# Attention at a quarter of its rate during the half-size products, from batch 2 on

## The chip, the cores and the metric

The kernel runs on one core of a Trainium2 chip. The metric is the device time of one execution in microseconds, as a median of several runs. The work is spread over five engines, each with its own queue of instructions that it goes through in order: PE (TensorE, the matmuls; its weight loads are shown apart as PEld), DVE (VectorE), ACT (ScalarE), POOL (GpSimd), and SP, which issues most of the DMA transfers.

## What is computed

Sigmoid attention over 8 batches, 12 heads, 448 positions and a head size of 64, and behind it a two-layer network over the 3584 tokens:

```python
scores = scale * np.matmul(q, k.transpose(0, 1, 3, 2)) - np.log(S)
attn = 1.0 / (1.0 + np.exp(-scores))
attn_out = np.matmul(attn, v)
x = attn_out.transpose(0, 2, 1, 3).reshape(B * S, H * D)      # 3584 x 768
h = x @ w_in                                                  # 768 x 2048
g = np.where(h >= 1, h, np.where(h <= -1, 0.0, (h + 1) ** 2 / 4))
out = g @ w_out                                               # 2048 x 768
```

## The kernel before

**Precision.** From a certain point on every float32 operand is split into a high and a low float16 part, scaled by a power of two; a product is then three matmuls (high by high, high by low, low by high). A split is an ACT instruction for the high part and a DVE (or POOL) instruction for the low one.

**Attention** is cut into pieces. A pair of heads has 3 full pieces (128 keys) and a smaller one (64 keys), so a batch has 6 x 4 = 24 pieces. `step(i)` moves attention on: it issues the scores of pieces ahead (`scores`, L435, L430, L449, into a `psc` tile, of which there are two), the sigmoid of each and its split (`weigh`: L478 and L486 on ACT, L487 on DVE), and the matmuls with v for pieces whose sigmoids are older (`av`, L524). In the later batches two pieces go in one step. At the last piece of a head pair ACT copies the result to `x32` (L533) and DVE takes its maximum (L534). `step` also loads the inputs of a later head pair (`raw`, L329, issued by SP), takes their maxima on ACT (`dump`, L345) and splits them on POOL (L381 to L383).

**The network** of batch b runs while the attention of batch b + 1 does. From batch 2 on the first layer is done by seven products of half-size blocks for each of 8 pairs of output chunks (`up_blocks`, L718: 9 matmuls of 224 columns in a unit, 56 units). Sums and differences of the seven come from DVE (L727) and ACT (L730, L736), and `bend` makes the nonlinear function and its split (L765, L768 on ACT, L766, L767, L769 on DVE). The second layer (`down`, L788: 6 matmuls of 448 columns in a unit, 48 units, 288 matmuls a batch) has one eviction for every 48 matmuls (L801, DVE).

**Between two batches** the x operands have to be built from `x32`. `start_blocks` takes the maximum over the batch (L556) and sets it on a diagonal (`diag`, L163, DVE); `finish_blocks` sums that on PE (L173, into a `psc` tile), takes the maximum (L174, DVE), makes the scale (L129 to L137, DVE), the block differences (L567, L569 on DVE; L568, L570 on POOL), and seven splits (L573 on ACT, L574 on DVE) in the order of the products. The first half-size product of the next batch reads the first split's two parts.

**What sets the order.** The loop over the units of a batch (L941) runs attention steps ahead of a unit while fewer have been made than the unit's share; `share` is the running sum of a weight for each unit. Only the first `last` = 92 of 104 units have a share; ahead of the unit with number `last` stands `start_blocks`, and behind it `finish_blocks`. A scheduler then places the instructions of each engine by priority (the order in which the program issues them) and by when it estimates them to be ready, so that the matmuls of later units can stand ahead of an attention step whose inputs it expects late.

## Time and profile before

| | |
|---|---|
| median of 3 runs | 1179.57 us (1179.01 to 1179.93) |
| profiled execution | 1178.28 us |
| its span in the profile | 1176.4 us |
| granted PE clock, mean | 0.996 |
| half-size products of batch 3, in the trace | about 520 to 600 us |
| down products of batch 3, last ones without attention | about 600 to 658 us |
| half-size products of batch 7, no attention beside them | 1068 to about 1125 us |

A row of the timeline gives start and length in us, the engine, the line of the kernel, what is written and read, a count, and in brackets the idle time before it and what ended it. A row of the stretches gives each engine's busy time in the stretch, with its instructions in parentheses, then the granted PE clock (1.00 is full), the share of the DMA engines and their GB/s. A matmul's length includes the time in which it overlaps the next one. A row of the waits gives the engine and line that waited, the engine and line that ended the wait, the total in us, how often, and the longest. A "pair" in what follows is a step of two pieces; a "boundary" is the place between two batches' networks.

### The profile page before, as it was taken

The page shows a single profiled execution, that of the slowest core. Times are in us where ns is not written, and L with a number is a line of the kernel's source. Part 1 is how long each engine was busy: PE and PEld are TensorE (multiplying, and loading weights), DVE is VectorE, ACT ScalarE, POOL GpSimd, SP SyncE. Part 2 cuts the span into 40 slices and gives each one's busy share as a digit, 9 for nine tenths or more (in the row PEclk, how much of TensorE's full clock was granted, in tenths as well). Part 3 has the DMA queues.
Part 4 walks back from the last instruction along what each step waited for, and adds up shares of the span by engine and source line. Part 5 has one row for each costly group of instructions (what it writes and reads, how often), then busy time and mean ns, then how long its engine had stood idle before and what let it go on. Part 6 is the DMA issues. An engine that isn't in the chain of part 4 may idle for free.

```text
span 1176.4 us, 20214 instructions
## 1 busy us (share of the span) xinstructions
PE 1123.5 (96%) x7662; PEld 672.0 (57%) x7662; DVE 813.2 (69%) x1730; ACT 722.9 (61%) x1199; POOL 289.3 (25%) x367
## 2 busy tenths in 40 slices
PE   8899999999988999999999999999999999999998
PEld 2244334454444775468744786448754687558954
DVE  6888976769868786368854788357873688646820
ACT  6878977568656766447763777456864576533410
POOL 0000000000334533424244235232533342310000
PEclk9999999999999999999999999999999999999999
DMA  9924553162564554216633264414562255302300
GB/s 360 399 81 149 161 155 95 44 211 87 189 204 151 195 189 155 72 57 203 237 110 100 81 228 171 140 56 143 192 212 64 65 197 179 129 17 107 145 17 31
DMA packets 58273, 170.00 MB, mean 145 GB/s; under 512 B 8641, under 2 KB 40001, under 8 KB 52033
## 3 DMA queue, kind: packets, MB, share of 16 engines
q1 hardware_dynamic: 56448, 159.29, 39.7%
q10 hardware_dynamic: 1728, 9.44, 2.3%
q8 instruction: 60, 0.98, 0.3%
q14 instruction: 37, 0.29, 0.1%
HBM read 126.94 MB, written 23.40 MB: 128 GB/s over the span
## 4 chain that ended last, share of the span: by engine, by line
PE 48%; DVE 16%; ACT 14%; DMA 9%; issue 5%; POOL 5%; SPq 2%; POOLq 0%; DVEq 0%; ACTq 0%
PE po L788 24%; PE ph L718 9%; PE ph L752 6%; DMA raw<-qkv 5%; PE pav L524 5%; DVE ahl L487 4%; ACT psc L478 4%; DVE xhl L727 3%; ACT ahl L486 2%; DVE g L766 2%; PE psc L435 2%; DVE g L767 2%; DMA w_out_sb<-w_in 2%; ACT ghl L768 2%; ACT dump L345 2%
## 5 line engine op out<-in xcount | busy, mean ns | idle before, releaser
L788 PE MATMUL po<-ghl,w_out_sb 128*128 128x448 f16 x2304 | 445.4, 353 | 7.7 <-ACT ghl L768 6.3
L788 PEld LDWEIGHTS <-w_out_sb 128*128 128x128 f16 x2304 | 222.6, 98 | 223.0 <-issue 21.0
L718 PE MATMUL ph<-w_in_sb 128*128 128x224 f16 x3024 | 302.6, 260 | 19.9 <-DVE xhl L727 16.6
L718 PEld LDWEIGHTS <-w_in_sb 128*128 128x128 f16 x3024 | 287.4, 98 | 38.6 <-issue 35.4
L487 DVE SCALAR_TENSOR_TENSOR ahl<-psc,ahl 128x896 f16<-128x896 f32 (+1 forms) x170 | 153.1, 901 | 100.1 <-ACT ahl L486 98.3
L381 POOL TENSOR_SCALAR raw<-raw,qkv_s 128x448 f32<-128x448 f32 (+1 forms) x93 | 75.7, 827 | 455.2 <-DVE qkv_i L137 395.9
L478 ACT ACTIVATE psc<-psc,nls,sqk 128x896 f32<-128x896 f32 (+1 forms) x136 | 128.1, 966 | 54.6 <-PE psc L449 34.5
L486 ACT ACTIVATE ahl<-psc 128x896 f16<-128x896 f32 (+1 forms) x170 | 125.9, 763 | 38.4 <-DVE ahl L487 37.3
L345 ACT ACTIVATE dump<-raw 128x448 f16<-128x448 f32 (+1 forms) x105 | 61.9, 589 | 88.7 <-DMA raw<-qkv 87.6
L752 PE MATMUL ph<-xhl,w_in_sb 128*128 128x448 f16 x576 | 112.7, 353 | 3.6 <-ACT xhl L547 1.8
L768 ACT ACTIVATE ghl<-g 128x448 f16<-128x448 f32 x128 | 73.0, 573 | 59.7 <-DVE g L767 58.9
L769 DVE TENSOR_TENSOR ghl<-g,ghl 128x448 f16<-128x448 f32 x128 | 84.0, 659 | 33.2 <-ACT ghl L768 32.6
L727 DVE TENSOR_TENSOR xhl<-ph,xhl 128x224 f32<-128x224 f32 x240 | 87.1, 384 | 18.0 <-PE ph L718 12.8
L752 PEld LDWEIGHTS <-w_in_sb 128*128 128x128 f16 x576 | 55.1, 98 | 62.9 <-issue 11.1
L765 ACT ACTIVATE g<-xhl,hr,ihr 128x448 f32<-128x448 f32 x96 | 68.4, 756 | 35.8 <-DVE xhl L727 34.5
L524 PE MATMUL pav<-ahl,v 128*64 128x448 f16 x748 | 88.0, 360 | 0.0
L766 DVE SCALAR_TENSOR_TENSOR g<-g,rk 128x448 f32<-128x448 f32 x112 | 81.2, 735 | 8.2 <-ACT g L765 8.0
L801 DVE TENSOR_SCALAR o<-po,od 128x448 f32<-128x448 f32 x42 | 28.5, 680 | 73.4 <-PE po L788 73.2
L435 PE MATMUL psc<-qk 128*128 128x448 f16 x252 | 62.5, 357 | 8.8 <-DVE ahl L487 5.5
L383 POOL TENSOR_TENSOR hl<-raw,hl 128x448 f16<-128x448 f32 x62 | 67.7, 1112 | 0.0
L767 DVE SCALAR_TENSOR_TENSOR g<-xhl,ihs,g 128x448 f32<-128x448 f32 x96 | 66.8, 708 | 0.3
L458 POOL COPY w_in_sb<-hl 64x128 f16<-64x128 f16 x68 | 27.9, 411 | 142.2 <-DVE hl L377 140.2
(151 smaller groups left out, 1120.3 us busy)
## 6 DMA issues: line engine op xcount, KB each, us to landing
w_in_sb<-blocks SPq DMA_DIRECT2D x48, 1344.0 KB, 6.8
raw<-qkv SPq DMA_DIRECT2D x34, 704.0 KB, 4.5
qk<-hl SPq DMA_DIRECT2D x320, 56.0 KB, 2.0
w_out_sb<-w_in SPq DMA_DIRECT2D x16, 768.0 KB, 11.1
out_t<-o SPq DMA_DIRECT2D x48, 224.0 KB, 1.9
blocks<-mixs SPq DMA_DIRECT2D x8, 768.0 KB, 3.5
w_out_sb<-w_out ACTq DMA_DIRECT2D x6, 768.0 KB, 5.4
raww<-w_out ACTq DMA_DIRECT2D x6, 768.0 KB, 6.2
```

Source lines behind the costliest of these rows:

```text
L435: once(nc.tensor.matmul(out, kq[:, j, 1, w], kq[:, j, 0, :], start=True, stop=False))
L478: nc.scalar.activation(a, a, AF.Sigmoid, bias=nls, scale=sqk)
L486: nc.scalar.activation(hi, x, AF.Copy, scale=ATT)
L487: made.setdefault(i, []).append(nc.vector.scalar_tensor_tensor(out=lo, in0=x, scalar=ATT, in1=hi, op0=ALU.mult, op1=ALU.subtract))
L524: once(nc.tensor.matmul(pav[j * D : (j + 1) * D, :S], *terms[j][t], start=c == 0 and t == 0, stop=mid and t == len(terms[j]) - 1,))
L718: nc.tensor.matmul(out, w[:, wt, wh, c * P : (c + 1) * P], xc[:, xt, c, xh, :], start=j in (0, 2) and c + wh + xh == 0, stop=c == HC - 1 a ...
L727: add = lambda out, q, other: nc.vector.tensor_tensor(out=out, in0=quarter(q), in1=other, op=ALU.add)
L752: nc.tensor.matmul(ph[:, :S], w_in_sb[:, f, wh, c * P : (c + 1) * P], xhl[:, c, xh, :], start=c == 0 and wh + xh == 0, stop=c == NCC - 1 a ...
L766: nc.vector.scalar_tensor_tensor(out=g, in0=g, scalar=rt, in1=g, op0=ALU.min, op1=ALU.mult)
L767: nc.vector.scalar_tensor_tensor(out=g, in0=h, scalar=ihs, in1=g, op0=ALU.mult, op1=ALU.max)
L768: latest["g"] = nc.scalar.activation(hi, g, AF.Copy)
L788: nc.tensor.matmul(po[:, :S], w_out_sb[:, f, wh, m * P : (m + 1) * P], ghl[:, f, gh, :], start=f == lo and wh + gh == 0, stop=f == hi - 1 ...
```

## The change

The weight of a unit is now 2 instead of 8 for the first 56 units of each batch from 2 on, which are the units of the half-size products; the 36 down units behind them that have a share keep 8. Batches 0 and 1 are as they were.

```diff
-DW = 8
+DW, UW = 8, 2
...
-        share = [DW // 2 if b < SB and u < NA * NCC // 2 else DW for u in range(last)]
+        mixed_up = 7 * NFC // 2 if b >= SB else 0
+        share = [UW if u < mixed_up else DW // 2 if b < SB and u < NA * NCC // 2 else DW for u in range(last)]
         share = [sum(share[:u]) / sum(share) for u in range(last + 1)]
```

NFC is 16, SB is 2. No instruction is added or removed; the scheduler's order changes from batch 2 on.

PE around the boundary from batch 2 to batch 3, before: the last attention matmuls with v (L524), down matmuls (L788), the sum of the diagonal (L173), and more down matmuls.

```order
L524 MATMUL pav_4839<-ahl_4834,v_4483 64x448
...
L788 MATMUL po_4878<-ghl_94,w_out_sb_91 128x448
...
L788 MATMUL po_4997<-ghl_94,w_out_sb_91 128x448
L173 LDWEIGHTS one_96 [waits DVE_49]
L173 MATMUL psc_5033<-diag_5025,one_96 128x128 [waits PE_49]
L788 LDWEIGHTS w_out_sb_91
...
L788 MATMUL po_5131<-ghl_94,w_out_sb_91 128x448
...
L435 MATMUL psc_5185<-qk_4723 128x448 [waits PE_49]
```

Between the last L524 and L173 stood 50 down matmuls, and 63 between L173 and the next scores (L435); at the later boundaries 49, 49, 49 and 36 ahead of it and 53, 53, 53 and 66 behind it.

The same place now:

```order
L524 MATMUL pav_4885<-ahl_4880,v_4621 64x448
...
L435 MATMUL psc_4960<-qk_4787 128x448 [waits DVE_49]
...
L449 MATMUL psc_4960<-hl_4776 128x448
L173 LDWEIGHTS one_96 [waits DVE_49]
L173 MATMUL psc_5033<-diag_5025,one_96 128x128 [waits PE_49]
...
L435 MATMUL psc_5185<-qk_4787 128x448 [waits PE_49]
...
L524 MATMUL pav_5207<-ahl_4968,v_4777 64x448 [waits Activation_49]
...
L430 MATMUL psc_5188<-hl_4776,w_in_sb_90 128x448 [waits DVE_49]
...
L157 MATMUL psc_5188<-mb_5192,one_96 128x3
...
L718 MATMUL ph_5221<-w_in_sb_90 128x224 [waits Activation_49]
...
L718 MATMUL ph_5221<-w_in_sb_90 128x224 [waits DVE_49]
```

All 288 down matmuls of the batch now stand ahead of L173, and behind it stand only scores and matmuls with v of the next batch's first pieces, then the products, whose first matmuls wait for the first split (ACT for its high part, DVE for its low one). The scores of the batch's last two pieces stand 12 matmuls L524 and 26 matmuls L788 ahead of the last L524; at the next boundaries 34, 25, 11 and 7 matmuls L788.

DVE at the same place now:

```order
L534 TENSOR_REDUCE xm_3510<-x32_92 128x1 [waits Activation_49]
L569 TENSOR_TENSOR xhl_93<-x32_92,xhl_93 128x672
L556 TENSOR_REDUCE xm1_5023<-xm_3510 128x1 [waits DVE_49]
L487 SCALAR_TENSOR_TENSOR ahl_4968<-psc_4957,ahl_4968 128x896 [waits PE_49,Activation_49]
L163 TENSOR_SCALAR diag_5025<-ident_98,xm1_5023 128x128 [waits DVE_49]
L487 SCALAR_TENSOR_TENSOR ahl_4972<-psc_4960,ahl_4972 128x896 [waits PE_49,Activation_49]
L174 TENSOR_REDUCE xm1_5023<-psc_5033 128x1 [waits PE_49]
```

Both L487 of the next batch's first two pieces stand inside the chain from L534 to L174; before, one of them stood ahead of L556 and the other ahead of L534.

PE at the boundary from batch 6 to batch 7 now, where no next pieces exist:

```order
L788 MATMUL po_11818<-ghl_94,w_out_sb_91 128x448
...
L524 MATMUL pav_11627<-ahl_11618,v_11413 64x448 [waits Activation_49]
...
L173 LDWEIGHTS one_96 [waits DVE_49]
L173 MATMUL psc_11720<-diag_11712,one_96 128x128 [waits PE_49]
...
L718 MATMUL ph_11870<-w_in_sb_90 128x224 [waits Activation_49]
...
L718 MATMUL ph_11870<-w_in_sb_90 128x224 [waits DVE_49]
```

Before, 66 down matmuls stood between L173 and L718 here; now none.

## The prediction

> **What bounds the kernel now.** I read the page first, then stretches of the timeline, then TensorE's waits. The page:

> ```profile
> PE 1123.5 (96%) x7662; PEld 672.0 (57%) x7662; DVE 813.2 (69%) x1730; ACT 722.9 (61%) x1199; POOL 289.3 (25%) x367
> ```

> TensorE (PE) works 96% of the span. The change alters no instruction, only the order, so it can move nothing but PE's idle time and its clock. The stretches show where that idle time is: the half-size products of batch 3 (520 to 600 us), its down products while attention runs (604 to 645), the last down products (645 to 658), the next products, and those of batch 7, which have no attention beside them.

> ```profile
> core 0: us, PE busy (x) PEld busy (x) DVE busy (x) ACT busy (x) POOL busy (x), PEclk, DMA share, GB/s
> 520.00:600.00 80.00, 78.09 (x699) 61.16 (x696) 65.79 (x139) 58.73 (x104) 34.67 (x44) 1.00 0.51 174
> 604.00:645.00 41.00, 40.59 (x230) 19.99 (x230) 16.53 (x34) 19.09 (x31) 17.46 (x24) 1.00 0.25 75
> 645.00:658.00 13.00, 13.00 (x78) 6.62 (x75) 9.03 (x29) 8.64 (x15) 0.71 (x1) 1.00 0.18 69
> 1068.00:1125.00 57.00, 55.44 (x543) 51.81 (x542) 40.42 (x86) 23.90 (x46) 0.00 (x0) 1.00 0.34 126
> ```

> DVE is 82% busy in the products and 40% in the down products. The idea has a basis: attention sits where DVE is short. But PE loses only 1.9 of 80 us there. PE's waits from 360 us on, and four of its gaps:

> ```profile
> PE ph L718 <- DVE xhl L727: 16.6, 8, 5.7
> PE po L788 <- ACT ghl L768: 6.3, 4, 2.7
> PE ph L718 <- ACT xhl L736: 1.6, 1, 1.6
> PE ph L718 <- DVE g L766: 1.6, 1, 1.6
> PE po L788 <- DVE xhl L727: 0.9, 4, 0.2
> ...
> 379.98 1.84 PE L718 MATMUL ph<-w_in_sb 128*128 128x224 f16 x9 [5.65 <-DVE xhl L727]
> 412.44 3.46 PE L718 MATMUL ph<-w_in_sb 128*128 128x224 f16 x18 [2.35 <-DVE xhl L727]
> ...
> 604.29 8.77 PE L788 MATMUL po<-ghl,w_out_sb 128*128 128x448 f16 x44 [1.24 <-ACT ghl L768]
> ...
> 1091.24 25.19 PE L718 MATMUL ph<-w_in_sb 128*128 128x224 f16 x261 [1.56 <-DVE g L766]
> ```

> In all 27.0 us. The 5.65 at the start of batch 2 (the order ahead of it is the same in both kernels) and the 1.56 of batch 7 (no attention) stay, so **the most that thinner attention can win is 27.0 - 5.65 - 1.56 = 19.8 us**.

> **The change part by part.** Steps come in pairs of pieces. Before, 24 pieces spread evenly over 92 units: a pair every 7.7 units, 8 of 12 pairs in the 56 product units. Now the weights are 56x2 + 36x8 = 400: a pair every 16.7 units, then every 4.2 units, 4 pairs and 8. But the order does not follow: in the down products the scheduler sets 41 to 45 matmuls between pairs, as it did before, not the 25 that 4.2 units would be. So attention slips towards the end of the batch and uses up all 288 down matmuls. Before, 53 to 66 of them stood behind `diag` and covered the building of the next batch's x operands (copy, maxima, scale, splits). Now none do, at each of the five boundaries from 2->3 to 6->7. Down products with pairs 42 matmuls apart ran without a new gap in the 604 to 645 row, so I cost that density at nothing; its cover is exactly that spacing.

> *First wait at a boundary.* What covered this chain, and how long its parts last (boundary 3->4 of the kernel before):

> ```profile
> 624.29 0.36 PE L449 MATMUL psc<-hl 64*128 64x448 f16 x2
> 624.59 1.32 PE L524 MATMUL pav<-ahl,v 128*64 128x448 f16 x12
> 625.85 7.93 PE L788 MATMUL po<-ghl,w_out_sb 128*128 128x448 f16 x41
> 626.00 0.58 ACT L345 ACTIVATE dump<-raw 128x448 f16<-128x448 f32 x1 [7.52 <-DMA raw<-qkv]
> ...
> 628.03 1.67 ACT L478 ACTIVATE psc<-psc,nls,sqk 128x448 f32<-128x448 f32 x2
> ...
> 633.03 0.63 DVE L487 SCALAR_TENSOR_TENSOR ahl<-psc,ahl 64x448 f16<-64x448 f32 x1 [0.60 <-ACT ahl L486]
> ...
> 637.88 0.63 ACT L533 ACTIVATE x<-pav,sqk 128x448 f32<-128x448 f32 x1
> ...
> 645.46 10.19 PE L788 MATMUL po<-ghl,w_out_sb 128*128 128x448 f16 x53
> ```

> The scores of the last two pieces end at 624.65; the pieces are ready at 633.66, 9.0 us later, of which 3.4 go to the `dump` that waits for its load ahead of the sigmoids in ACT's queue. A down matmul costs 7.93/41 = 0.193 us. For the rest of the chain the trace has one near double, boundary 1->2, with the same DVE order, the two L487 of the next batch's pieces in it:

> ```profile
> 358.58 0.62 DVE L534 TENSOR_REDUCE xm<-x 128x1 f32<-128x448 f32 x1 [0.96 <-ACT x L533]
> ...
> 362.84 1.09 DVE L487 SCALAR_TENSOR_TENSOR ahl<-psc,ahl 128x896 f16<-128x896 f32 x1 [0.34 <-ACT ahl L486]
> ...
> 365.62 1.90 DVE L574 SCALAR_TENSOR_TENSOR w_in_sb<-x,x_s,w_in_sb 128x672 f16<-128x672 f32 x1
> 367.56 0.90 DVE L574 SCALAR_TENSOR_TENSOR w_in_sb<-xhl,x_s,w_in_sb 128x672 f16<-128x672 f32 x1
> ...
> 368.98 5.35 PE L718 MATMUL ph<-w_in_sb 128*128 128x224 f16 x54
> ...
> 373.98 0.20 DVE L582 TENSOR_SCALAR qq<-qm 128x1 f32<-128x1 f32 x1
> ```

> From L534 to the end of the first L574 it took 8.9 us; with that L574 at 0.9, as its successor, 7.9. With the copy L533 (0.6 and 0.1 to pass on) the first product can run 8.6 us after the last attention matmul.

> - 2->3: behind the last scores stand 12 attention matmuls and 26 down matmuls, 1.3 + 5.0 = 6.3 us; then a half pair of scores and six of the ten last attention matmuls, about 1.3 together; the other four must wait for 9.0: 1.4 us idle. Then 8.6 us of chain, under which stand only the next pieces' scores and 12 attention matmuls, about 3.7 us: 4.9 idle. Together 6.3.
> - 4->5, 25 down matmuls: 6.5. 3->4, 34 of them: no first part, 4.9. 5->6, only 11: 15 fewer, 2.9 more than the first: 9.2.
> - 6->7: no next load and no next pieces. Ready 5.6 us from the sigmoids on (628.03 to 633.66) against 1.3 + 7x0.193 + 0.7 = 3.4: 2.2 idle; chain 8.6 less the two L487 and their wait, 2.5, so 6.1 bare. 8.3.

> Sum 35.2 us. From below: if the next pieces' L487 slip behind the chain and the load is early, 6.1 - 3.7 = 2.4 four times and 6.1 once, 16. From above: the load as late as at its worst in the waits of ACT, 8.8 instead of 7.5 us, and an L574 of 1.9 each time, some 45. I keep 35, from the near double.

> ```profile
> ACT dump L345 <- DMA raw<-qkv: 81.2, 15, 8.8
> ```

> *Second wait.* From the end of the first L574 (367.52) the six other splits and the scales keep DVE until 374.18, 6.7 us; behind them stand the two L487 of the next pieces and the L727 on which the fifth product waits, some 2 us more; PE's 54 matmuls last 5.35. So PE waits again, up to 3.4 us, and 1.5 at 6->7, where no L487 is. One L727 now stands ahead of the L487, which helps. Bounds: 0, and the 5.65 us of batch 2. I take 3 four times and 1.5: 13.5.

> *The clock.* After the gap of 5.65 us PE came back slow:

> ```profile
> 378.00:380.00 2.00, 0.02 (x1) 0.02 (x1) 1.94 (x12) 1.36 (x5) 0.00 (x0) 0.60 0.00 0
> 380.00:382.00 2.00, 2.00 (x11) 1.45 (x10) 1.91 (x8) 0.58 (x3) 0.00 (x0) 0.50 0.00 0
> 382.00:384.00 2.00, 2.00 (x10) 0.66 (x10) 0.69 (x6) 1.12 (x2) 1.51 (x3) 0.50 0.03 8
> 384.00:386.00 2.00, 2.00 (x12) 0.54 (x9) 0.23 (x1) 1.07 (x3) 2.00 (x4) 0.69 0.00 0
> ...
> 414.00:416.00 2.00, 2.00 (x12) 1.51 (x10) 0.90 (x4) 0.00 (x0) 0.00 (x0) 0.51 0.49 197
> ```

> The granted clock was 0.50, 0.50 and 0.69 over six us: 1.0 + 1.0 + 0.6 = 2.6 us lost. Five boundaries: 13; from 0 to twice that, if the second wait slows it once more.

> [...]

> *What is won.* Up to 19.8 us, and 2 of clock behind the 2.35 us gap. The order has 5 pairs in the products where there were 8: six pieces of about 1.1 us on DVE each, 6.6 of its 65.8 us, go. Batch 7 shows that gaps remain even without attention (1.56), and the gap at 604.29 comes of a load. I take two thirds: 13.

> Sum against the profiled execution (span 1176.4, with 1.9 around it 1178.3): +35.2 + 13.5 + 13 - 13 = +48.7. The median of the three runs is 1.3 above that execution: **1179.6 + 48.7 = 1228 us**.

> **The rivals.**
> *Faster.* The chain shrinks to its lower bound at all boundaries, 16 us, the second wait is hidden under the products' 5.35 us, the clock drops only at 6->7 (2.6), and 21.8 are won: -3, 1176 us. It decides for itself only if a boundary costs less than 4 us. For it: the pieces' 9.0 us contain 3.4 of waiting for a load. Against: the first product's matmuls wait for ACT and DVE in the order with nothing but attention ahead, and 1->2 shows the chain at its length. 0.05.
> *Deeper.* With more pairs in the down products the loads arrive later each time, ACT stands before `dump` up to 8.8 us with the sigmoids behind it, and the second wait is 5.65 each time: +10 + 15 + 8 of clock on the forecast, 1260. For it: 81.2 us of such waits on ACT already. Against: the spacing that sets them is unchanged. 0.14.
> *It doesn't do what it says.* The weights shift pairs that the scheduler puts back by readiness, and waits move but don't grow: 1179 to 1181. Against: 8 pairs became 5 and `diag` moved behind all down products. 0.05.
> *Mild.* ACT and DVE, with less of the products to serve, run ahead and halve the waits and the clock's loss: +17.9, 1197. For it: DVE's 40% in the down products. Against: the chain is a series of steps, each waiting for the last, not a queue that a freer engine shortens. 0.06.

> **How the numbers follow.** The forecast keeps 0.70. Its terms reach from 1200 (first waits 25, second 5, clock 8, 17 won) to 1250 (45, 22, 18, 15 won). The range is 1194 to 1254, which takes in the mild case and half of the deeper one; what it leaves out is the 0.05 and 0.05 below and some 0.08 above. A change under 0.2% (2.4 us) can't be told from none: faster 0.05, same 0.05, slower 0.90.

> **What would show it.** Right: in the changed profile five places, each behind the last down matmul of a batch, where L718 waits for ACT L573 or DVE L574, 5 to 9 us with the waits of L524 ahead; granted clock near 0.5 behind each; down products still full; the L727 gaps of the products fewer. Wrong: if those places show under 3 us, the chain was overpriced; if the down products get gaps, the spacing was no cover; if the product gaps stay, nothing was won.

## The result, and the profile after

| | before | after |
|---|---|---|
| median of 3 runs | 1179.57 us (1179.01 to 1179.93) | 1221.65 us (1218.87 to 1222.61) |
| profiled execution | 1178.28 us | 1218.87 us |
| its span | 1176.4 us | 1217.1 us |
| PE busy / idle in the span | 1123.5 / 52.9 us | 1136.8 / 80.3 us |
| granted PE clock, mean | 0.996 | 0.980 |

The change makes the kernel slower: after over before is 1.0352, with an interval of 1.0325 to 1.0379. The prediction was 1228 us with a range of 1194 to 1254.

The page of the kernel after, PE's busy time and the granted clock in 40 slices of the span:

```profile
PE 1136.8 (93%) x7662; PEld 671.8 (55%) x7662; DVE 834.2 (69%) x1730; ACT 723.4 (59%) x1199; POOL 291.5 (24%) x367
...
PEclk9999999999999999899998999999999799998999
```

The number of matmuls is the same, 7662. PE's busy time has still grown by 13.3 us, and its idle time by 27.4; together they are the 40.7 us of the spans. A slice is 30 us wide; the clock's dips stand in those that begin at 487, 639, 943 and 1095 us, which hold four of the five boundaries.

PE's waits from 360 us on, after (engine and line that waited, what ended the wait, us in total, times, longest):

```profile
PE psc L173 <- DVE diag L163: 16.7, 4, 4.9
PE psc L435 <- DVE ahl L487: 10.6, 7, 5.3
PE ph L718 <- DVE xhl L727: 10.1, 10, 1.8
PE pav L524 <- DVE ahl L487: 7.7, 2, 4.4
PE ph L718 <- ACT xhl L736: 3.5, 8, 0.6
PE ph L718 <- DMA w_in_sb<-blocks: 2.4, 3, 1.6
PE ph L718 <- ACT w_in_sb L573: 1.8, 1, 1.8
PE ph L718 <- DVE w_in_sb L574: 1.1, 2, 0.6
```

L173, L435 and L524 were not in this list before; now they have the longest waits. They are the maximum's matmul, the scores of the next pieces and the matmuls with v, all of them at a boundary. The waits for L727 inside the products have become shorter, 10.1 us against 16.6, and no wait of the down products (L788) is left in the list, where there were 6.3 and 0.9.

The longest gaps at four of the five boundaries in the timeline of PE, after:

```profile
508.49 0.29 PE L173 MATMUL psc<-diag,one 128*128 128x128 bf16 x1 [4.34 <-DVE diag L163]
...
654.24 2.45 PE L524 MATMUL pav<-ahl,v 128*64 128x448 f16 x12 [4.41 <-DVE ahl L487]
659.71 5.24 PE L718 MATMUL ph<-w_in_sb 128*128 128x224 f16 x53 [0.51 <-DVE w_in_sb L574]
...
946.65 0.93 PE L435 MATMUL psc<-qk 128*128 128x448 f16 x2 [5.34 <-DVE ahl L487]
955.36 0.29 PE L173 MATMUL psc<-diag,one 128*128 128x128 bf16 x1 [3.95 <-DVE diag L163]
...
1097.60 1.14 PE L524 MATMUL pav<-ahl,v 128*64 128x448 f16 x10 [3.34 <-DVE ahl L487]
1103.65 0.29 PE L173 MATMUL psc<-diag,one 128*128 128x128 bf16 x1 [4.92 <-DVE diag L163]
1105.77 0.35 PE L718 MATMUL ph<-w_in_sb 128*128 128x224 f16 x1 [1.83 <-ACT w_in_sb L573]
```

The brackets hold the idle time ahead of each row. Up to the first split's matmuls, and with the short gaps that are not shown, they add up to 5.05 us at 2->3, 4.92 at 3->4, 5.96 at 4->5, 10.0 at 5->6 and 10.7 at 6->7: **36.6 us**. In the first products behind them there are 4.9 us more, 0.45 to 2.29 a boundary. All other idle time from 360 us on is 12.6 us; it was 27.0.

The clock fell at all five boundaries. The first five rows are the stretches there in which it stood at 0.50 (from and to, length, PE's busy time with its matmuls, the clock, the share of the DMA engines, GB/s). The last row is a piece of the down products ahead of the second boundary, with the columns of the prediction (PE, PEld, DVE, ACT and POOL, then the clock). After:

```profile
508.44:515.27 6.83, 6.07 (x27) 0.50 0.42 131
651.80:658.62 6.82, 4.38 (x19) 0.50 0.58 173
801.98:805.40 3.42, 3.42 (x17) 0.50 0.30 67
945.34:962.41 17.07, 11.10 (x46) 0.50 0.29 83
1098.94:1109.18 10.24, 3.09 (x16) 0.50 0.00 0
...
600.00:640.00 40.00, 40.00 (x236) 19.81 (x236) 14.48 (x30) 18.01 (x32) 14.38 (x22) 1.00 0.27 83
```

PE was busy for 28.1 us at 0.50 there. Twelve matmuls L524 took 2.45 us at 654.24, against 1.32 at full clock before (624.59), so I estimate the loss at half of the 28.1 us: 14.0, or 2.8 a boundary. Before the change PE was busy for 8.7 us at 0.50, behind two gaps of batch 2 (378.40 to 385.22 and 412.53 to 415.94 us); these 4.3 us are no longer lost. So the 13.3 us by which PE's busy time grew are +14.0 at the boundaries, -4.3 in batch 2, and 3.6 that these rows don't hold; 1.5 of the 3.6 are a stretch at half clock at 338 us, ahead of batch 2. The down products are full, 40.00 of 40 us.

So the time went here: waits up to the first product +36.6, in the first products +4.9, PE's busy time +13.3, other waits -14.4. The sum is +40.4 against the 40.7 of the spans.

### The profile page after: what moved, and what is told of

Same layout as the page of the kernel before. It is cut to its first block, busy times and chain, and to the rows that moved or that the text cites. A ratio compares the mean times of both kernels' runs of the same rounds, so it can differ in the third digit from the quotient of the medians.

```text
span 1217.1 us, 20256 instructions
## 1 busy us (share of the span) xinstructions
PE 1136.8 (93%) x7662; PEld 671.8 (55%) x7662; DVE 834.2 (69%) x1730; ACT 723.4 (59%) x1199; POOL 291.5 (24%) x367
## 4 chain that ended last, share of the span: by engine, by line
PE 52%; DVE 15%; ACT 12%; DMA 9%; issue 6%; POOL 4%; SPq 2%; POOLq 0%; DVEq 0%; ACTq 0%
PE po L788 20%; PE ph L718 16%; PE ph L752 6%; PE pav L524 6%; DMA raw<-qkv 3%; DVE ahl L487 3%; DMA w_out_sb<-w_in 3%; PE psc L435 2%; ACT psc L478 2%; ACT dump L345 2%; DVE w_in_sb L574 2%; ACT ahl L486 2%; PE psc L449 2%; DVE g L766 1%; DVE g L767 1%
## 5 line engine op out<-in xcount | busy, mean ns | idle before, releaser
L788 PE MATMUL po<-ghl,w_out_sb 128*128 128x448 f16 x2304 | 446.2, 353 | 0.0
L788 PEld LDWEIGHTS <-w_out_sb 128*128 128x128 f16 x2304 | 221.7, 98 | 216.6 <-issue 15.3
L718 PE MATMUL ph<-w_in_sb 128*128 128x224 f16 x3024 | 304.8, 260 | 19.1 <-DVE xhl L727 10.1
L718 PEld LDWEIGHTS <-w_in_sb 128*128 128x128 f16 x3024 | 287.9, 98 | 37.7 <-issue 30.8
L487 DVE SCALAR_TENSOR_TENSOR ahl<-psc,ahl 128x896 f16<-128x896 f32 (+1 forms) x170 | 152.8, 899 | 120.7 <-ACT ahl L486 114.2
L381 POOL TENSOR_SCALAR raw<-raw,qkv_s 128x448 f32<-128x448 f32 (+1 forms) x93 | 68.4, 749 | 503.1 <-DVE qkv_i L137 349.6
L478 ACT ACTIVATE psc<-psc,nls,sqk 128x896 f32<-128x896 f32 (+1 forms) x136 | 128.3, 967 | 85.2 <-PE psc L449 62.1
L486 ACT ACTIVATE ahl<-psc 128x896 f16<-128x896 f32 (+1 forms) x170 | 126.8, 762 | 36.5 <-DVE ahl L487 34.8
L768 ACT ACTIVATE ghl<-g 128x448 f16<-128x448 f32 x128 | 72.7, 575 | 67.8 <-DVE g L767 67.2
L727 DVE TENSOR_TENSOR xhl<-ph,xhl 128x224 f32<-128x224 f32 x240 | 85.9, 383 | 24.7 <-PE ph L718 22.7
L345 ACT ACTIVATE dump<-raw 128x448 f16<-128x448 f32 (+1 forms) x105 | 61.9, 590 | 68.2 <-DMA raw<-qkv 67.0
L524 PE MATMUL pav<-ahl,v 128*64 128x448 f16 x748 | 93.0, 376 | 7.7 <-DVE ahl L487 7.7
L766 DVE SCALAR_TENSOR_TENSOR g<-g,rk 128x448 f32<-128x448 f32 x112 | 86.6, 788 | 14.9 <-ACT g L765 14.5
L769 DVE TENSOR_TENSOR ghl<-g,ghl 128x448 f16<-128x448 f32 x128 | 80.8, 643 | 10.3 <-ACT ghl L768 9.8
L435 PE MATMUL psc<-qk 128*128 128x448 f16 x252 | 65.7, 365 | 18.4 <-DVE ahl L487 16.0
L767 DVE SCALAR_TENSOR_TENSOR g<-xhl,ihs,g 128x448 f32<-128x448 f32 x96 | 74.3, 794 | 0.2
L383 POOL TENSOR_TENSOR hl<-raw,hl 128x448 f16<-128x448 f32 x62 | 71.7, 1175 | 0.0
L458 POOL COPY w_in_sb<-hl 64x128 f16<-64x128 f16 x68 | 34.8, 512 | 141.8 <-DVE hl L377 139.9
```

What stands on the lines that cost most here:

```text
L345: ins = nc.scalar.activation(dump[:, : rt.shape[1]], rt, AF.Abs, accum_out=m[:, t : t + 1])
L435: once(nc.tensor.matmul(out, kq[:, j, 1, w], kq[:, j, 0, :], start=True, stop=False))
L478: nc.scalar.activation(a, a, AF.Sigmoid, bias=nls, scale=sqk)
L486: nc.scalar.activation(hi, x, AF.Copy, scale=ATT)
L487: made.setdefault(i, []).append(nc.vector.scalar_tensor_tensor(out=lo, in0=x, scalar=ATT, in1=hi, op0=ALU.mult, op1=ALU.subtract))
L524: once(nc.tensor.matmul(pav[j * D : (j + 1) * D, :S], *terms[j][t], start=c == 0 and t == 0, stop=mid and t == len(terms[j]) - 1,))
```

## The experiments

Times are medians; "before" was run beside each group on the same chip (1179.7, 1179.5 and 1180.7 us). In the order that the kernels give, I call **cover** the down matmuls that stand between the last attention matmul of a batch's own pieces and the first product of the next batch. They stand in two places: ahead of the maximum's matmul (L173) and behind it.

| kernel | cover ahead, 2->3 to 6->7 | cover behind | us | ratio to before |
|---|---|---|---|---|
| before | 50, 49, 49, 49, 36 | 63, 53, 53, 53, 66 | 1179.6 | |
| changed (weight 2) | 0, 0, 0, 0, 0 | 0, 0, 0, 0, 0 | 1221.65 | 1.0352 |
| weight 4 | 46, 31, 46, 43, 33 | 0, 0, 0, 0, 10 | 1191.21 | 1.0097 |
| weight 5 | 50, 48, 41, 44, 33 | 17, 5, 0, 0, 46 | 1178.7 | 1.0001 |
| weight 6 | 48, 48, 48, 48, 33 | 35, 35, 35, 35, 50 | 1172.68 | 0.9948 |
| old rate, all cover ahead | 113, 97, 97, 97, 89 | 0, 0, 0, 0, 0 | 1207.54 | 1.0236 |
| old rate, last two pairs late | 0, 0, 0, 0, 0 | 0, 0, 0, 0, 0 | 1240.55 | 1.0522 |

### The last down matmuls held behind the maximum's matmul

```diff
-                nc.tensor.matmul(
+                ins = nc.tensor.matmul(
...
+                if held:                 # units past LAST - 48 of batches 2 to 6
+                    behind(ins, "diag")  # L173
```

> The changed kernel, with the last 11 down units (66 matmuls) of batches 2 to 6 kept behind the diagonal's sum on PE, as they stood before the change; nothing is left out. Theory A (what costs is only that the cover was used up): with 66 matmuls, 12.7 us, behind L173 again the waits at the boundary (36.6 us ahead of the first product and 4.9 in it, in the changed kernel's trace) and most of the clock's 13 us go: 1222 - 45 or so, 1165 to 1180. Theory B (pairs of pieces can't follow each other faster in the down products than ACT, DVE and the two psc tiles let them, some 10 us a pair, so the cover was the filler of that time): PE stands idle ahead of the last scores and matmuls with v instead, some 4 + 6.5 + 4 us a boundary with 2 matmuls where 42 stood: slower than the changed kernel, 1230 to 1255.

Measured: 1241.3 us (1238.5 to 1244.33), ratio 1.0536 (1.0505 to 1.0566). PE's longest waits from 360 us on:

```profile
PE psc L435 <- DVE ahl L487: 40.7, 10, 6.1
PE psc L173 <- DVE diag L163: 14.5, 5, 4.9
```

The products hardly wait any more (L727: 1.1 us), but the scores do, 40.7 us of it. At each boundary there are now three gaps, such as 4.01, 5.85 and 2.39 us, and PE's busy time is 1152.4 us. The 66 matmuls that were put behind L173 had stood between the last pairs, where they filled the time that a pair takes from its scores to its sigmoids. This is theory B. Cover can't be got by moving the same matmuls within an end that holds too much attention: what is late is the attention.

### Filling matmuls in the gap

```diff
+WARM = 60
...
     def finish_blocks(xm1, diag, warm=0):
+        for n in range(warm):      # 64 columns each, behind L533, into columns that nothing reads
+            ins = nc.tensor.matmul(state["pav"][:, S:], ones, ident[:, : 512 - S], start=True, stop=True)
```

> The changed kernel, with 60 matmuls of 64 columns added at each boundary from batch 2 on, behind the copy of the last attention result and ahead of L173, into columns that nobody reads; they add nothing to the result. If the slow clock behind the boundary's gap is a cost of its own (PE's busy time grew by 13.3 us with no instruction added): the waits of PE stay at some 37 us less the time of the added matmuls, which run inside the wait, the granted clock stays nearer to 1 behind them, and the time falls by 4 to 10 us to 1212 to 1218. If the clock's loss is not caused by the gap, or if it hides under the same chain (DVE and ACT set the first products' time whatever PE's clock): 1222 within 3.

Measured: 1213.31 us (1209.68 to 1214.71), ratio 1.0289 (1.0265 to 1.0314), 8.3 us less than the changed kernel. The clock at 2->3 (three rows of PE alone), and at 3->4 (all engines):

```profile
510.51:513.92 3.41, 1.96 (x15) 1.00 0.25 56
520.75:524.16 3.41, 1.17 (x12) 1.00 0.00 0
524.16:527.58 3.42, 3.42 (x20) 0.50 0.01 2
...
656.00:660.00 4.00, 4.00 (x26) 1.47 (x25) 1.06 (x2) 2.80 (x4) 4.00 (x7) 0.50 0.09 21
```

Behind the gap at 2->3 the clock stayed at 1.00, where it had been 0.50; it fell 13 us later, behind waits of 1.80 and 0.45 us in the first products. At 3->4 it fell as before; there the longest gap (4.46 us) stands ahead of the last scores and not where the filling stands. From 360 us on PE was busy for 24.7 us at 0.50, against 28.1 in the changed kernel, which is some 1.7 us won by the estimate above. PE was busy for 1150.0 us in all, 10.1 of them with the filling; the 1139.9 that are left are not fewer than the 1136.8 of the changed kernel, but some 3.4 of them were lost at 0.50 at 53 and 138 us, where the changed kernel's trace has full clock. So the time came out where it was expected, but the trace carries little of the reason: most of the 8 us came out of idle time. That the clock's loss is a cost of its own rests on the 0.50 rows and on PE's busy time, not on this run.

### The new weights in batch 2 alone

```diff
-        mixed_up = 7 * NFC // 2 if b >= SB else 0
+        mixed_up = 7 * NFC // 2 if b == SB else 0
```

> The new weights in batch 2 alone. Theory by terms: one boundary (2->3) is left, 5.05 + 0.45 us of waits and some 2.9 of clock in the changed kernel's trace, and batch 2's own gaps shrink from 12.2 us to 2.3, with 4.6 us of slow clock behind them gone: 1179.6 + 8.4 - 14.5, 1173 (1170 to 1177), so faster than before. Rival (each batch costs its fifth of the 42 us): 1188.

Measured: 1176.27 us (1174.3 to 1179.13), ratio 0.9976 (0.9961 to 0.999). One boundary is bare (2->3, gaps of 4.35 and 0.72 us); batch 2's own gaps, 12.2 us before, are some 2.5. In that one batch the gain is a little larger than one bare boundary costs, because before the change batch 2 had nearly half of all gaps. The later batches had little to win.

### Weight 6 instead of 2

```diff
-DW, UW = 8, 2
+DW, UW = 8, 6
```

> The weight of the product units 6 instead of 2 (before: 8), for batches 2 to 7. In the order 35 down matmuls stand behind L173 at the boundaries, and 50 at the last: 6.8 us, with the next scores and matmuls with v some 9 us. Theory of the cover: no wait at a boundary over 1 us, the product gaps a little fewer than before: 1172 to 1180. Rival (thinner attention in the products costs by itself, in proportion to the weight, a third of the way from 8 to 2): 1193.

Measured: 1172.68 us (1171.04 to 1173.55), ratio 0.9948 (0.993 to 0.9966): faster than before. PE's waits from 360 us on are chiefly these:

```profile
PE ph L718 <- DVE xhl L727: 10.5, 6, 5.5
PE ph L718 <- ACT xhl L736: 6.4, 5, 1.3
```

The longest, 5.5 us, is the gap at the start of batch 2. None of the others, nor the 1.0 us for a weight load that is left, is at one of the five boundaries from 2->3 on. A mild thinning of attention wins in the products and keeps its cover.

### Weights 5 and 4

```diff
-DW, UW = 8, 2
+DW, UW = 8, 5
```

> The changed kernel with weight 5 instead of 2 for the product units. The order now leaves 17, 5, 0, 0 and 46 down matmuls behind the maximum's matmul at the boundaries 2->3 to 6->7 (weight 6: 35, 35, 35, 35, 50; weight 2: none). Theory (cover): a boundary without cover costs what it cost in the changed kernel, 36.6 + 4.9 of waits and 13.3 of clock over five = 11.0 us each; 17 matmuls cover 3.3 us and leave one gap of some 4 us with its clock, 5; 5 matmuls leave 9; 46 leave none. 5 + 9 + 11 + 11 + 0 = 36 over the 1172.7 of weight 6: about 1208 us, with waits of 5 us and more at 4->5 and 5->6 and none at 6->7. Rival (the rate): the loss grows with how much attention the products lose, evenly from weight 6 (1172.7) to weight 2 (1221.7): weight 5 is 1185 us, and 6->7 waits like the others.

> The changed kernel with weight 4. The order leaves 0, 0, 0, 0 and 10 down matmuls behind the maximum's matmul. Cover: four boundaries at 11.0 us and one at about 8, 52 over the 1172.7 of weight 6: about 1220 to 1225 us, the same as weight 2 within 0.5%, although twice as much attention stays in the products. Rate: half way between weight 6 and weight 2, 1197 us.

Measured: weight 5 1178.7 us (1176.21 to 1183.04), ratio 1.0001 (0.9985 to 1.0017); weight 4 1191.21 us (1190.56 to 1192.61), ratio 1.0097 (1.0076 to 1.0117). Both expectations missed: cover, as I had counted it, said 1208 and over 1220; the even rate said 1185 and 1197. I had counted only what stands behind L173. The table shows what that left out: with weights 4 and 5 there are 31 to 50 down matmuls ahead of L173 and behind the last own attention matmul, and these hide the copy and the maximum just as well. PE at boundary 3->4 with weight 4:

```profile
651.76 0.23 PE L173 MATMUL psc<-diag,one 128*128 128x128 bf16 x1
...
654.60 0.26 PE L718 MATMUL ph<-w_in_sb 128*128 128x224 f16 x1 [1.25 <-ACT w_in_sb L573]
655.55 6.90 PE L718 MATMUL ph<-w_in_sb 128*128 128x224 f16 x53 [0.70 <-DVE ru L582]
663.28 0.93 PE L718 MATMUL ph<-w_in_sb 128*128 128x224 f16 x8 [0.82 <-DVE xhl L727]
```

L173 doesn't wait. What is left is the part behind it, the scale and the first splits: 1.25 + 0.70, and 0.82 in the first products. At the five boundaries this adds up to 2.77, 2.77, 2.77, 3.57 and 1.80, 13.7 us. PE's busy time is 5.0 us over that of before, and the other waits from 360 us on 7.3 under theirs: +11.4 of the 13.4 us between the two spans. The other 2.0 are idle time ahead of 360 us or in gaps too short for the list. So I formed a second reading: cover ahead of L173 pays for the copy and the maxima, cover behind it for the scale and the splits. The next two runs test it with the old rate of attention in the products.

### The end alone: the last two pairs late, all else at the old rate

```diff
-        last = len(units) - 96 + LAST
+        last = len(units) - 96 + (LAST if b < SB else 95)
...
         share = [sum(share[:u]) / sum(share) for u in range(last + 1)]
+        if b >= SB:
+            share = [min(u / 92, 20 / NPIECE) for u in range(last)] + [1.0]
```

> The kernel before, with its own rate of attention in the products, but the last two pairs of each batch from 2 to 6 held back to the batch's end: no down matmul is left between the batch's last attention matmul and the next batch's first product, as in the changed kernel, while 66, 66, 54, 54 and 54 of 132 attention matmuls stay in the products (before 66 each, changed 44, 44, 44, 32, 32). 12 down matmuls stand ahead of the last scores' pair where the changed kernel has 26, 34, 25, 11 and 7. Cover: the waits of the changed kernel, 36.6 and 4.9 us with 13.3 of clock, 0.193 us for each of the about 43 matmuls fewer ahead of the last pair, 8, and nothing won in the products: 1179.6 + 63 = 1242 us, not under 1230. Rival (the loss comes of products with thin attention, or of pairs crowded into the down products): the time stays within 10 us of 1180.

Measured: 1240.55 us (1240.02 to 1243.24), ratio 1.0522 (1.0494 to 1.0551). The boundary 2->3:

```profile
518.41 0.90 PE L435 MATMUL psc<-qk 128*128 128x448 f16 x2 [1.96 <-DVE ahl L487]
...
526.14 0.29 PE L173 MATMUL psc<-diag,one 128*128 128x128 bf16 x1 [3.49 <-DVE diag L163]
...
538.62 3.63 PE L718 MATMUL ph<-w_in_sb 128*128 128x224 f16 x34 [1.22 <-DVE xhl L727]
```

These are the gaps of the changed kernel, in a kernel whose products kept at least 54 of the 66 attention matmuls of before. Up to the first product the gaps add up to 34.4 us (changed: 36.6), in the first products to 4.1 (4.9). The loss therefore needs no thin attention in the products; a bare boundary is enough. The sum was met, but not by its terms: the 8 us for fewer matmuls ahead of the last pairs did not come, PE's busy time grew by 22.1 us (to 1145.6) instead of 13.3, about 16.7 of them lost at the boundaries at a clock of 0.50 (half of 33.4 us busy), and other idle time grew by 5.0, with 9.2 us of waits for weight loads.

### All cover ahead of the maximum's matmul

```diff
+            share = [min(u / 92, 23 / NPIECE) for u in range(last)] + [1.0]
```

with `last` as in the run above.

> The kernel before, with the same rate, but the maximum's matmul and what hangs on it moved to the batch's end: 113, 97, 97, 97 and 89 down matmuls stand between the batch's last attention matmul and the maximum's matmul, and none behind it (before: 50, 49, 49, 49, 36 ahead and 63, 53, 53, 53, 66 behind). First reading (only what stands behind the maximum's matmul covers): as bare as the changed kernel, 1220 us or more. Second reading (down matmuls ahead of it cover the copy and the maxima, those behind it the scale and the splits): no wait at the maximum's matmul; behind it 7 scores' and 12 attention matmuls, about 3.1 us, against scale and first splits, so 0.7 to 1.3 us ahead of the first product and 1.9 to 2.5 ahead of the fifth, as with weight 4: 2.6 to 3.8 us at each of five boundaries, 1179.6 + 15 = about 1195 us. Third (any order with enough down matmuls behind the last attention is as good): 1180 us.

Measured: 1207.54 us (1204.58 to 1212.32), ratio 1.0236 (1.0191 to 1.0281). Boundary 3->4, and the first wait for a weight load behind it:

```profile
661.98 0.22 PE L173 MATMUL psc<-diag,one 128*128 128x128 bf16 x1
...
665.98 5.24 PE L718 MATMUL ph<-w_in_sb 128*128 128x224 f16 x53 [0.92 <-DVE w_in_sb L574]
672.86 5.14 PE L718 MATMUL ph<-w_in_sb 128*128 128x224 f16 x52 [1.64 <-DVE xhl L727]
...
692.97 7.29 PE L718 MATMUL ph<-w_in_sb 128*128 128x224 f16 x46 [3.72 <-DMA w_in_sb<-blocks]
```

The first reading falls: L173 waits at no boundary. The second is right on the boundaries: 2.56, 2.56, 2.57, 2.56 and 2.98, 13.2 us where 15 was expected and weight 4 had 13.7. It is wrong on the sum, 1207.5 instead of 1195: the products now wait 17.9 us for weight loads, which no reading had foreseen, and PE's busy time is 13.2 us higher, about 5 of them lost at a clock of 0.50 ahead of 360 us. The load that PE awaits at 692.97 was issued by SP at 684.64 and landed at 692.93; that is 19.8 us from the start of the products (664.80) to its issue, where it was 13.3 before (658.08 to 671.35). In SP's queue it stands behind the loads of the next head pair (L390, L391), and these wait for GpSimd's split (L382), which began at 679.00 here and at 665.72 before.

### GpSimd beside the maximum

In the changed kernel L163, the instruction that L173 waits for, is slow. DVE and GpSimd at 2->3 and at 6->7, after:

```profile
506.79 1.59 POOL L568 TENSOR_TENSOR xhl<-x 128x672 f32<-128x672 f32 x1
506.92 1.51 DVE L163 TENSOR_SCALAR diag<-ident,xm 128x128 bf16<-128x128 bf16 x1
...
1099.55 1.60 POOL L568 TENSOR_TENSOR xhl<-x 128x672 f32<-128x672 f32 x1 [35.95 <-ACT x L533]
1099.98 1.89 DVE L569 TENSOR_TENSOR xhl<-x,xhl 128x672 f32<-128x672 f32 x1
...
1101.95 1.60 POOL L570 TENSOR_TENSOR xhl<-x,xhl 128x672 f32<-128x672 f32 x1 [0.79 <-DVE xm L556]
1101.97 1.62 DVE L163 TENSOR_SCALAR diag<-ident,xm 128x128 bf16<-128x128 bf16 x1
```

The same place in the kernel before, 3->4:

```profile
641.97 0.25 DVE L163 TENSOR_SCALAR diag<-ident,xm 128x128 bf16<-128x128 bf16 x1
```

Beside that one GpSimd ran a copy of 64x128 (L458, from 641.83 us), so "nothing ran there beside it" in the expectation below is wrong. Nor is the long L163 new: it took 0.65 and 0.92 us at 2->3 and 6->7 before, hidden by the cover.

At 2->3 L163 ends at 508.43 and L568 at 508.38; at 6->7 L163 ends at 1103.59 and L570 at 1103.55. The run puts the two subtractions of GpSimd on DVE:

```diff
-TP = 1
+TP = 0
```

> The changed kernel with the two subtractions of L568 and L570 on DVE instead of GpSimd. In the changed kernel diag (L163) took 1.51 us on DVE while L568 ran on GpSimd, and 0.25 in the kernel before, where nothing ran there beside it; L569 took up to 2.05 against 0.85. Theory (DVE is slowed beside GpSimd at an uncovered boundary): L163 takes 0.25 to 0.5 at all five, the first wait is shorter by about 1 us each; on the other hand DVE has two subtractions of about 0.9 us more ahead of the splits, so that the second wait grows by up to 1.8 where they stand in the path. Sum -5 to +4: 1217 to 1226 us; L163 decides the point, not the time. Rival (L163 was long for another reason, a semaphore or a matmul it shares a buffer with): it stays above 0.9 us at two or more boundaries.

Measured: 1222.08 us (1219.51 to 1223.31), ratio 1.0354 (1.0331 to 1.0376), no different from the changed kernel. At 6->7, with nothing on GpSimd:

```profile
1106.49 0.85 DVE L569 TENSOR_TENSOR xhl<-x,xhl 128x672 f32<-128x672 f32 x1
...
1107.38 0.86 DVE L570 TENSOR_TENSOR xhl<-x,xhl 128x672 f32<-128x672 f32 x1
1108.15 0.25 DVE L163 TENSOR_SCALAR diag<-ident,xm 128x128 bf16<-128x128 bf16 x1
```

L163 took 0.24 to 0.28 us at all five boundaries and L569 0.85 here; at three others, beside GpSimd's splits (L383), L569 took 1.68. So the point is decided: they were slow because GpSimd was working. The time shows no gain, since the two subtractions now stand ahead of L163 on DVE itself and take what it had waited; L173's waits are 22.4 us instead of 16.7.

### Thin attention at the start of batch 2, weight 6 from batch 3 on

```diff
-        mixed_up = 7 * NFC // 2 if b >= SB else 0
-        share = [UW if u < mixed_up else DW // 2 if b < SB and u < NA * NCC // 2 else DW for u in range(last)]
+        mixed_up = 10 if b == SB else 7 * NFC // 2 if b > SB else 0
+        share = [(UW if b == SB else 6) if u < mixed_up else DW // 2 if b < SB and u < NA * NCC // 2 else DW for u in range(last)]
```

> A version meant to keep what the change won without its price: in batch 2 weight 2 for the first 10 units and 8 for the rest, from batch 3 on weight 6 for the product units. The order leaves 35, 35, 35, 35 and 50 down matmuls behind the maximum's matmul, as with weight 6 throughout, and thins attention at the start of batch 2, where weight 6 keeps a gap of 5.50 us. Cover, and gaps that come of DVE's backlog: no wait of more than 1.5 us at a boundary, batch 2's gap falls to about 1 to 2 us with 2.6 of clock behind it, so 1172.7 - 4 - 2.6 = 1166 us, against 1179.6 for the kernel before. Rival (the gap of batch 2 belongs to a load that comes late whatever attention does): the gap stays, and the time is that of weight 6, 1172 to 1173.

Measured: 1170.97 us (1165.82 to 1173.22), ratio 0.9921 (0.9897 to 0.9944). PE's longest waits from 360 us on:

```profile
PE ph L718 <- DVE xhl L727: 8.6, 8, 2.4
PE ph L718 <- ACT xhl L736: 5.1, 4, 1.3
```

No boundary from 2->3 on has a wait ahead of its first product; 1.70 us are left in the first products at 2->3, a little over the 1.5 allowed. The 5.50 us gap at the start of batch 2 is 1.22 and 0.72; so it did hang on attention. Of the 6.7 us expected below weight 6 only 1.7 came, and the two overlap in their runs (1171.04 to 1173.55): that this is faster than before is shown, that it is faster than weight 6 is not.

## Why the prediction was right, by its steps

**Only idle time and clock can move.** Right in the main: same instructions, idle +27.4, busy +13.3; 2.1 of the 13.3 are in no row at half clock.

**The first waits, 35.2.** Measured 36.6: 5.05 for 6.3, 4.92 for 4.9, 5.96 for 6.5, 10.0 for 9.2 and 10.7 for 8.3. The run with the end alone changed has 34.4 with the old rate in the products, so the cause is the bare end, as the step had it. In sum its two parts were right as well: ahead of the last own attention matmuls 9.5 us were forecast and 10.4 came, for the chain behind them 25.7 and 26.2. Two things in it were wrong. The cover it named, "53 to 66 of them stood behind `diag`", was half of what was lost; 36 to 50 more stood ahead of it, and the cover ahead alone hides most: with it 13.2 and 13.7 us were left of 41.5. No run has the cover behind alone with attention on time. And the place was wrong. For the chain's part the step let PE stand at the first product, and "what would show it" named L718 waiting for L573 or L574; that is 2.9 us of the 36.6. PE stands at L173, at scores, and at matmuls with v. In the chain, L163 and L569 were mostly longer than in the near double (0.96 and 0.85 us). At 6->7 they took 1.62 and 1.89 beside GpSimd, 1.7 us more; the chain left 7.4 us bare there against 6.1. The rest of what the 8.3 fell short of 10.7 came ahead of the last own matmuls, 3.3 against 2.2.

**The second wait, 13.5.** This is the term that was mis-sized: 4.9. Both bounds of the step were kept, but the value was taken too near to the 1->2 row. The step counted "some 2 us more" for two L487 and the L727 behind the splits and scales. In the trace the first L727 stands ahead of both L487 at the four boundaries that have them, and it starts 5.5 to 7.9 us behind the end of the first L574, where 6.7 + 2 was counted; the step had seen this ("which helps") and not taken it off. Another part is that two terms overlap: PE comes slowly out of the gap, so the first products begin and end later and need L727 later. They began 1.6 and 2.3 us behind the first split at 2->3 and 5->6. Where the clock stayed at 1.00, at 2->3 in the run with filling matmuls, the second wait was 1.80 + 0.45 against 0.45.

**The clock, 13.** By the rows at 0.50, 14.0, or 2.8 a boundary; PE's busy time, +13.3, also holds what was no longer lost in batch 2. The trace bears out the row that the step took, 2.6 us behind one gap. In the run with late pairs, with three or more gaps close together at each boundary, it was 16.7.

**What is won, 13 of at most 19.8 and 2 of clock.** Measured 14.4 us of waits and 4.3 of clock, 18.7; the term was 5.7 too small. 3.75 of the 14.4 come from the gap at the start of batch 2 (5.65, now 1.18 + 0.72) that the step said would "stay", and 2.6 of the 4.3 from the half clock behind it. Without that gap 10.7 and 1.7 were won, 12.4 together, close to the 13. The step looked at PE's order ahead of that gap, but its cause was on ACT. ACT there, before:

```profile
375.59 0.58 ACT L345 ACTIVATE dump<-raw 128x448 f16<-128x448 f32 x1 [3.97 <-DMA raw<-qkv]
...
376.17 1.32 ACT L486 ACTIVATE ahl<-psc 128x896 f16<-128x896 f32 x2
...
377.95 0.34 ACT L730 ACTIVATE xhl<-ph 128x224 f32<-128x224 f32 x1
```

And after:

```profile
371.14 1.34 ACT L486 ACTIVATE ahl<-psc 128x896 f16<-128x896 f32 x2
372.37 0.34 ACT L730 ACTIVATE xhl<-ph 128x224 f32<-128x224 f32 x1
```

Before, ACT stood 3.97 us at a `dump` whose load was late, and the split (L486) and the product's copy (L730) that PE and DVE needed stood behind it. With attention thinned, that `dump` comes later in ACT's queue. With weight 6 throughout the gap was 5.50 still; with 2 for the first ten units of batch 2 it went.

**No cost for pairs 42 matmuls apart.** Right: 40.00 of 40 us busy.

**The rivals.** "Mild" and "faster" needed shorter first waits; none was under 4.9 us. "It doesn't do what it says" falls with the order itself. "Deeper" needed later loads and a second wait of 5.65 each; it was 1.0 on average.

So the sum, +48.7 against +40.4 by these terms (40.7 by the spans), was high by 8.3: the second wait was 8.6 too much and what is won 5.7 too little, against 1.4 too little in the first waits, 1.0 in the clock and 3.6 of busy time that no term had. That the last three took back 6.0 of the 14.3 us is luck; the first waits and the clock, which carry the forecast, are not.

## What to carry to other kernels

When the rate of a background task is lowered in one stage, look at where it then ends: here the order pushed the rest to the very end of the batch, and the work that had hidden the hand-over to the next batch was used up. Count such cover from the last instruction that the hand-over needs to the first that needs its result, on both sides of the steps in between, and price a bare hand-over with the clock that PE loses behind it (here 8.3 us of waits and about 2.8 us of clock). The gaps that the change was to remove were worth 27 us in all, nearly half of them in batch 2. A mild weight of 6 won (0.995), and so did weight 6 with the start of batch 2 thinned (0.992); the two can't be told apart.
